# First row chunks of x as 64-row halves over two DMA queues, turned by half transposes, in a SwiGLU feed-forward kernel

## Chip, cores and metric

The kernel runs on one core of one Trainium2 chip. The metric is the device time of one execution in microseconds (us). The profiler's "span" runs from the first to the last instruction of the program; the time is a little longer than the span. Engines are called as in the profile: PE is TensorE's matmuls, PEld its weight loads, DVE is VectorE, ACT is ScalarE, POOL is GpSimd, SP is SyncE. SPq and ACTq are the DMA queues that SP and ACT issue to.

## What is computed

```python
# x: (1, 2048, 640), w_gate, w_up: (640, 1536), w_down: (1536, 640), all bf16
g = silu(x @ w_gate)
u = x @ w_up
return (g * u) @ w_down
```

## The kernel before

Rows of x are taken in four blocks of 512 (`S_BLK`), the 640 columns of x in five slices of 128 (`KD`, index `kd`), the 1536 hidden columns in twelve slices of 128 (`KF`, index `fc` or `kf`). The gate and up products need x with its columns on the partitions, which is the tile `xT`. For block `sb` and slice `fc`, `proj` (L202) runs five matmuls into a gate tile `pg` and five into an up tile `pu`, each 512 rows wide; `gate` (L217) takes the silu on ACT and the product on DVE into `aT`. After the twelve slices the down product reads `aT` and `wd_sb` (L287 and L316) and the result is copied and stored. PE runs these in the order of the program text, since `keep_order` (L100) ties all its instructions together; ACT, POOL, DVE and SP are ordered likewise.

The part that the change touches is the start, `head` (L226), and the loads ahead of it.

**Loads.** Only the first 256 rows of x, two chunks of 128 rows (`PE_X = 2`), are loaded as they are and turned on PE; rows 256 to 511 and the other blocks come turned by the DMA itself (`turn_x`, L110). Chunk 0 goes over SPq and chunk 1 over ACTq (L114, L115), 160 KB each. Then come the gate weights of the first four `fc` slices (`N_FIRST = 4`), one transfer of 128 KB for each `kd` (L120 to L122): `kd` 1 and 3 over ACTq (`ACT_K`), 0, 2 and 4 over SPq. After them SPq takes the up weights of the same four slices, `kd` 0 to 2 in one transfer of 384 KB and `kd` 3 and 4 in one of 256 KB (L123, L124), the two turning transfers for rows 256 to 511 (L125, L126), and the weights of the other slices (L128 to L131).

**PE in `head`.** First `warm` (L180) issues 20 matmuls of 128x128 on a tile of ones (`N_WARM`); their result is not used. Then `transpose_chunk` (L190) turns chunk 0 and chunk 1: five 128x128 transposes each (L195), the x tile as the weights and the identity as what streams. The transposes of `kd` 0 and 1 fill one PSUM tile, which ACT copies into `xT`; those of `kd` 2 to 4 fill another, which DVE copies (L200). Then come the gate pieces (L246 to L256). A piece is one `kd` and a range of rows, and each piece is four matmuls, one for each `fc`: `kd` 0 on chunk 0 (128 rows), `kd` 0 on chunk 1 (128 rows), then `kd` 1, 2, 3 and 4 on both chunks at once (256 rows). That makes 8 matmuls of 128 rows and 16 of 256. The up matmuls on the same 256 rows follow, 20 of them, in order of `kd` (L257 to L259); then gate and up on rows 256 to 511, which need the turning transfers (L260 to L265).

The up weights are called by their first transfer below: the 384 KB of `kd` 0 to 2 are what the first up matmul waits for.

Of the kernel before, what the change touches and what calls it, by code (L numbers as in the profile page):

```python
# [10 lines left out]
def _body(  # L11
# [8 lines left out]
    nc = tc.nc  # L20
    P = nc.NUM_PARTITIONS
    f32 = mybir.dt.float32
    bf16 = mybir.dt.bfloat16
# [9 lines left out]
    KD = D // P  # L33
# [3 lines left out]
    SUB = S_BLK // P  # L37
    DA = 512
    Q = 32
    N_WARM = 20  # L40
    T = 4
    WT_STEP = 4
    PE_X = 2
    ACT_K = (1, 3)
    X_CUT = 3
    N_FIRST = 4
    ROW_J = 0
# [6 lines left out]
    psum = ctx.enter_context(  # L54
        tc.tile_pool(name="psum", bufs=2, space=bass.MemoryType.PSUM)
    )

    ident = consts.tile([P, P], bf16)
    x_sb = consts.tile([P, PE_X, D], bf16)
    xT = consts.tile([P, KD, S], bf16)  # L60
# [14 lines left out]
    x_v = x2.rearrange("(c p) d -> p c d", p=P)  # L75
# [5 lines left out]
    def wslice(a, b):  # L81
        return slice(a * P, b * P)
# [4 lines left out]
    def load_x(eng, c0, c1):  # L87
        eng.dma_start(out=x_sb[:, c0:c1, :], in_=x_v[:, c0:c1, :])
# [11 lines left out]
    def keep_order(engine):  # L100

        traced = [i for i in nc.cur_bb.bb.instructions if i.engine == engine]
        for a, b in zip(traced, traced[1:]):
            issue_order(a, b)
# [6 lines left out]
        s_sl = slice(c0 * P, c1 * P)  # L111
        nc.sync.dma_start_transpose(out=xT[:, k0:k1, s_sl], in_=xt_v[s_sl, k0:k1])

    load_x(nc.sync, 0, 1)  # L114
    load_x(nc.scalar, 1, 2)  # L115
    def load_k(eng, dst, src, a, b, k0, k1):
        f_sl = wslice(a, b)
        eng.dma_start(out=dst[:, k0:k1, f_sl], in_=src[:, k0:k1, f_sl])

    for kd in range(KD):  # L120
        eng = nc.scalar if kd in ACT_K else nc.sync
        load_k(eng, wg_sb, wg_v, 0, N_FIRST, kd, kd + 1)  # L122
# [12 lines left out]
    def turn_w(dst, src):  # L135
# [7 lines left out]
        out=x_row[:],  # L143
        in_=x2[S - T : S, :].rearrange("t d -> (t d)").partition_broadcast(P),
# [35 lines left out]
    def warm(n):  # L180
        for _ in range(n):
            nc.tensor.matmul(  # L182
                pw[:, 0:P],
                lhsT=ones[:].broadcast_to([P, P]),
                rhs=ones[:].broadcast_to([P, P]),
                start=True,
                stop=True,
            )

    def transpose_chunk(c, parts):  # L190
        c_sl = slice(c * P, (c + 1) * P)
        for copy, tag, k0, k1 in parts:
            pt = psum.tile([P, k1 - k0, P], bf16, tag=tag, name="pt")
            for kd in range(k0, k1):
                nc.tensor.transpose(  # L195
                    out=pt[:, kd - k0, :],
                    in_=x_sb[:, c, kd * P : (kd + 1) * P],
                    identity=ident[:],
                )
            copy(out=xT[:, k0:k1, c_sl], in_=pt[:])  # L200

    def proj(ps, w_sb, fc, sb, c0, c1, k0=0, k1=KD):  # L202
        for kd in range(k0, k1):
            nc.tensor.matmul(  # L204
                ps[:, c0:c1],
                lhsT=w_sb[:, kd, fc * P : (fc + 1) * P],
                rhs=xT[:, kd, sb * S_BLK + c0 : sb * S_BLK + c1],
                start=(kd == 0),
                stop=(kd == KD - 1),
            )  # L210
# [6 lines left out]
    def gate(pg, pu, sb, fc, n_s):  # L217

        s0 = sb * S_BLK
        sg = work.tile([P, S_BLK], f32, name="sg")  # L220
        nc.scalar.activation(sg[:, 0:n_s], pg[:, 0:n_s], ACT.Silu)  # L221
        nc.vector.tensor_tensor(  # L222
            out=aT[:, fc, s0 : s0 + n_s], in0=sg[:, 0:n_s], in1=pu[:, 0:n_s], op=ALU.mult
        )

    def head():  # L226

        dve, act = nc.vector.tensor_copy, nc.scalar.copy
        split = [(act, "po_a", 0, 2), (dve, "po_b", 2, KD)]
        late = PE_X * P
        pgs = [
            psum.tile([P, S_BLK], f32, tag="gu", name="pg", bufs=4)
            for _ in range(N_FIRST)
        ]
        warm(N_WARM)
        transpose_chunk(0, split)  # L240
        transpose_chunk(1, split)
        pus = [
            psum.tile([P, S_BLK], f32, tag="po_a" if fc % 2 == 0 else "po_b", name="pu")
            for fc in range(N_FIRST)
        ]
        pieces = [(0, c * P, (c + 1) * P) for c in range(PE_X)]  # L246
        pieces += [(kd, 0, late) for kd in range(1, KD)]
        for kd, c0, c1 in pieces:
            for fc, pg in enumerate(pgs):
                nc.tensor.matmul(  # L250
                    pg[:, c0:c1],
                    lhsT=wg_sb[:, kd, wslice(fc, fc + 1)],
                    rhs=xT[:, kd, c0:c1],
                    start=(kd == 0 and c0 == 0),
                    stop=(kd == KD - 1),
                )  # L256
        for kd in range(KD):  # L257
            for fc, pu in enumerate(pus):
                proj(pu, wu_sb, fc, 0, 0, late, kd, kd + 1)  # L259
        for k0, k1 in ((0, X_CUT), (X_CUT, KD)):  # L260
            for fc, pg in enumerate(pgs):
                proj(pg, wg_sb, fc, 0, late, S_BLK, k0, k1)
        for fc, (pg, pu) in enumerate(zip(pgs, pus)):
            proj(pu, wu_sb, fc, 0, late, S_BLK)
            gate(pg, pu, 0, fc, S_BLK)  # L265
        keep_order(mybir.EngineType.PE)
        keep_order(mybir.EngineType.Activation)
        keep_order(mybir.EngineType.Pool)

    head()  # L270
    for sb in range(NSB):
        n_s = S_BLK if sb < NSB - 1 else S_BLK - T
# [26 lines left out]
        for q in range(P // Q):  # L299
            nc.scalar.dma_start(  # L300
                out=out2[
                    sb * S_BLK : sb * S_BLK + n_t, DA + q * Q : DA + (q + 1) * Q
                ].rearrange("(i r) c -> r i c", r=Q),
                in_=ot_q[q * Q : (q + 1) * Q, :].rearrange("r (i c) -> r i c", c=Q),
            )

        for j in range(SUB):
            s0 = sb * S_BLK + j * P
# [4 lines left out]
            for c0, c1, tag in cols:  # L313
# [10 lines left out]
                if c1 < D:  # L324
                    nc.scalar.copy(ot[:], po[:])  # L325
                    eng = nc.sync
                else:
                    nc.vector.tensor_copy(out=ot[:], in_=po[:])  # L328
                    eng = nc.sync
# [81 lines left out]
def kernel(tc, *args):  # L411
    _body(tc, *args)
    tc.close()
    tc.compile()
    _trim(tc.nc)
# [30 lines left out]
```

## Time and profile before

| what | value |
|---|---|
| time, median of 3 runs (lowest to highest) | 163.4 us (163.05 to 163.59) |
| time of the profiled execution | 163.25 us |
| span of the profiled execution | 161.9 us |
| PE busy | 159.6 us, 818 matmuls |
| DVE busy | 110.5 us |
| ACT busy | 42.6 us |
| DMA | 15.86 MB, of it 6.25 MB in the first 20 us |

The 1.35 us between span and time lie ahead of the first and behind the last instruction of the program. In a line of the chain or of the timeline the first number is the start in us from the beginning of the span and the second the length in us; "x4" is the number of instructions merged in the line. In a line of groups the figures behind the bar are the busy time in us, the mean duration of one instruction in ns, and the idle time of the engine ahead of them. A line of DMA issues ends with the time from issue to landing in us. A matmul's duration contains its way through the array, so that the matmuls of a stream overlap in the records: what one of them costs is the distance from start to start. A window of the timeline shows whatever runs in it, with the start of the first.

### The profile page before, as it was taken

The page shows a single profiled execution, that of the slowest core. Times are in us where ns is not written, and L with a number is a line of the kernel's source. Part 1 is how long each engine was busy: PE and PEld are TensorE (multiplying, and loading weights), DVE is VectorE, ACT ScalarE, POOL GpSimd, SP SyncE. Part 2 cuts the span into 40 slices and gives each one's busy share as a digit, 9 for nine tenths or more (in the row PEclk, how much of TensorE's full clock was granted, in tenths as well). Part 3 has the DMA queues.
Part 4 walks back from the last instruction along what each step waited for, and adds up shares of the span by engine and source line. Part 5 has one row for each costly group of instructions (what it writes and reads, how often), then busy time and mean ns, then how long its engine had stood idle before and what let it go on. Part 6 is the DMA issues. An engine that isn't in the chain of part 4 may idle for free.

```text
span 161.9 us, 2159 instructions
## 1 busy us (share of the span) xinstructions
PE 159.6 (99%) x818; PEld 79.9 (49%) x818; DVE 110.5 (68%) x249; ACT 42.6 (26%) x74; POOL 0.6 (0%) x6
## 2 busy tenths in 40 slices
PE   9999999999999999999999999999999999999995
PEld 9885444444444444444444444444444444445454
DVE  1006223599469999989919999979964999993000
ACT  5032222112222222211222322221214222222121
POOL 1000000000000000000000000000000000000000
PEclk9999999999999999999999999999999999999999
DMA  7999999995089992003110000000310000000212
GB/s 228 280 345 348 363 209 241 230 190 100 32 186 139 241 225 58 0 0 34 65 65 4 0 0 2 0 0 4 64 66 32 0 0 0 0 4 0 52 37 73
DMA packets 41209, 15.86 MB, mean 98 GB/s; under 512 B 33264, under 2 KB 41072, under 8 KB 41200
## 3 DMA queue, kind: packets, MB, share of 16 engines
q1 hardware_dynamic: 32832, 14.81, 38.0%
q10 hardware_dynamic: 8368, 0.92, 3.7%
q8 instruction: 6, 0.10, 0.3%
q14 instruction: 3, 0.02, 0.1%
HBM read 6.88 MB, written 2.62 MB: 59 GB/s over the span
## 4 chain that ended last, share of the span: by engine, by line
PE 99%; DVE 0%; issue 0%
PE pu L204 32%; PE pg L204 31%; PE po_a L316 26%; PE po_t L287 6%; PE pg L250 2%; PE pw L182 1%; PE pt L195 1%; DVE ot_b L328 0%; DVE ones L108 0%
## 5 line engine op out<-in xcount | busy, mean ns | idle before, releaser
L204 PE MATMUL pu<-xT,wu_sb 128*128 128x512 bf16 (+2 forms) x260 | 59.3, 362 | 0.0
L204 PE MATMUL pg<-xT,wg_sb 128*128 128x512 bf16 (+2 forms) x240 | 56.9, 370 | 0.0
L222 DVE TENSOR_TENSOR aT<-sg,pu 128x512 bf16<-128x512 f32 (+1 forms) x48 | 32.5, 682 | 32.8 <-PE pu L204 32.8
L221 ACT ACTIVATE sg<-pg 128x512 f32<-128x512 f32 (+1 forms) x48 | 28.4, 597 | 71.1 <-PE pg L204 67.5
L316 PE MATMUL po_a<-wd_sb,aT 128*128 128x512 bf16 (+2 forms) x216 | 42.8, 358 | 0.0
L153 DVE SCALAR_TENSOR_TENSOR prod<-wgT,x_row 128x640 f32<-128x640 bf16 x48 | 39.4, 821 | 1.1
L153 DVE SCALAR_TENSOR_TENSOR prod<-wuT,x_row 128x640 f32<-128x640 bf16 x48 | 39.4, 822 | 1.0
L204 PEld LDWEIGHTS <-wu_sb 128*128 128x128 bf16 x260 | 25.4, 98 | 26.5 <-DMA wu_sb<-in_w_up_dram 0.2
L204 PEld LDWEIGHTS <-wg_sb 128*128 128x128 bf16 x240 | 23.5, 98 | 25.9
L316 PEld LDWEIGHTS <-aT 128*128 128x128 bf16 x216 | 20.7, 98 | 21.6
L325 ACT CAST ot<-po_a 128x512 bf16<-128x512 f32 (+1 forms) x17 | 9.5, 561 | 32.0 <-PE po_a L316 20.9
L287 PE MATMUL po_t<-aT,wd_sb 128*128 128x512 bf16 (+1 forms) x48 | 10.4, 366 | 0.0
L287 PEld LDWEIGHTS <-wd_sb 128*128 128x128 bf16 x48 | 4.7, 98 | 5.1
L328 DVE CAST ot_b<-po_a 128x128 bf16<-128x128 f32 x1 | 0.3, 292 | 9.9 <-PE po_a L316 9.9
L296 ACT CAST ot_t<-po_t 128x512 bf16<-128x512 f32 (+1 forms) x4 | 2.2, 559 | 11.6 <-PE po_t L287 11.6
L153 DVE DVE_READ_ACCUMULATOR prod<-wuT,x_row 128x1 f32 x48 | 4.0, 82 | 0.0
L153 DVE DVE_READ_ACCUMULATOR prod<-wgT,x_row 128x1 f32 x48 | 3.9, 82 | 0.0
L298 DVE STREAM_TRANSPOSE ot_q<-ot_t 128x512 bf16<-128x512 bf16 (+1 forms) x4 | 2.7, 678 | 1.7 <-ACT ot_t L296 1.7
L250 PE MATMUL pg<-xT,wg_sb 128*128 128x256 bf16 (+1 forms) x24 | 3.1, 307 | 0.0
L200 DVE COPY xT<-pt 128x384 bf16<-128x384 bf16 x2 | 0.7, 358 | 3.2 <-PE pt L195 3.2
L250 PEld LDWEIGHTS <-wg_sb 128*128 128x128 bf16 x24 | 2.6, 127 | 0.3
L182 PE MATMUL pw<-ones 128*128 128x128 bf16 x20 | 2.3, 313 | 0.3 <-DVE ones L108 0.3
(15 smaller groups left out, 8.0 us busy)
## 6 DMA issues: line engine op xcount, KB each, us to landing
wd_sb<-in_w_down_dram SPq DMA_DIRECT2D x1, 1920.0 KB, 14.6
out_dram<-ot SPq DMA_DIRECT2D x15, 128.0 KB, 1.7
wg_sb<-in_w_gate_dram SPq DMA_DIRECT2D x2, 640.0 KB, 6.7
wu_sb<-in_w_up_dram SPq DMA_DIRECT2D x2, 640.0 KB, 8.0
x_row<-in_x_dram SPq DMA_DIRECT2D x1, 640.0 KB, 4.9
wg_sb<-in_w_gate_dram SPq DMA_DIRECT2D x3, 128.0 KB, 3.5
wu_sb<-in_w_up_dram SPq DMA_DIRECT2D x1, 384.0 KB, 4.7
out_dram<-ot_q ACTq DMA_DIRECT2D x12, 32.0 KB, 2.1
```

Of the source, the lines that this page charges most:

```text
L153: nc.vector.scalar_tensor_tensor(out=prod[:], in0=wT[:, fc, :], scalar=1.0, in1=x_row[:, t, :], op0=ALU.mult, op1=ALU.mult, accum_out=acc[ ...
L182: nc.tensor.matmul(pw[:, 0:P], lhsT=ones[:].broadcast_to([P, P]), rhs=ones[:].broadcast_to([P, P]), start=True, stop=True,)
L195: nc.tensor.transpose(out=pt[:, kd - k0, :], in_=x_sb[:, c, kd * P : (kd + 1) * P], identity=ident[:],)
L204: nc.tensor.matmul(ps[:, c0:c1], lhsT=w_sb[:, kd, fc * P : (fc + 1) * P], rhs=xT[:, kd, sb * S_BLK + c0 : sb * S_BLK + c1], start=(kd == 0 ...
L221: nc.scalar.activation(sg[:, 0:n_s], pg[:, 0:n_s], ACT.Silu)
L222: nc.vector.tensor_tensor(out=aT[:, fc, s0 : s0 + n_s], in0=sg[:, 0:n_s], in1=pu[:, 0:n_s], op=ALU.mult)
L250: nc.tensor.matmul(pg[:, c0:c1], lhsT=wg_sb[:, kd, wslice(fc, fc + 1)], rhs=xT[:, kd, c0:c1], start=(kd == 0 and c0 == 0), stop=(kd == KD ...
L287: nc.tensor.matmul(po_t[:], lhsT=wd_sb[:, kf, DA:D], rhs=aT[:, kf, sb * S_BLK : sb * S_BLK + n_t], start=(kf == 0), stop=(kf == KF - 1),)
L296: nc.scalar.copy(ot_t[:], po_t[:])
L298: nc.vector.transpose(out=ot_q[:], in_=ot_t[:])
L316: nc.tensor.matmul(po[:], lhsT=aT[:, kf, s0 : s0 + P], rhs=wd_sb[:, kf, c0:c1], start=(kf == 0), stop=(kf == KF - 1),)
L325: nc.scalar.copy(ot[:], po[:])
```

## The change

The two chunks are loaded as four transfers of 80 KB: of each chunk, rows 0 to 63 over SPq and rows 64 to 127 over ACTq. Gate weight `kd` 3 moves from ACTq to SPq. `transpose_chunk` now issues, for each `kd`, two transposes, one for each half of 64 rows; the halves stand in different row halves of the array (`tile_position` 0 and 64) and fill one PSUM tile each, of 5 x 64 columns. ACT copies the first half's tile into `xT`, DVE the second's, each after all five `kd`. The gate pieces are now `kd` 0 and `kd` 1 on chunk 0, `kd` 0 and `kd` 1 on chunk 1 (16 matmuls of 128 rows), then `kd` 2 to 4 on both (12 of 256 rows). 17 warm matmuls are issued in place of 20.

```diff
-    N_WARM = 20
+    N_WARM = 17
...
-    ACT_K = (1, 3)
+    ACT_K = (1,)
...
-    load_x(nc.sync, 0, 1)
-    load_x(nc.scalar, 1, 2)
+    for c in range(PE_X):
+        for eng, r0 in ((nc.sync, 0), (nc.scalar, P // 2)):
+            r_sl = slice(r0, r0 + P // 2)
+            eng.dma_start(out=x_sb[r_sl, c, :], in_=x_v[r_sl, c, :])
...
-    def transpose_chunk(c, parts):
-        c_sl = slice(c * P, (c + 1) * P)
-        for copy, tag, k0, k1 in parts:
-            pt = psum.tile([P, k1 - k0, P], bf16, tag=tag, name="pt")
-            for kd in range(k0, k1):
+    def transpose_chunk(c, copies):
+        h_rows = P // len(copies)
+        pts = [
+            psum.tile([P, KD, h_rows], bf16, tag=tag, name="pt") for _, tag in copies
+        ]
+        for kd in range(KD):
+            for h, pt in enumerate(pts):
+                h_sl = slice(h * h_rows, (h + 1) * h_rows)
                 nc.tensor.transpose(
-                    out=pt[:, kd - k0, :],
-                    in_=x_sb[:, c, kd * P : (kd + 1) * P],
-                    identity=ident[:],
+                    out=pt[:, kd, :],
+                    in_=x_sb[h_sl, c, kd * P : (kd + 1) * P],
+                    identity=ident[h_sl, h_sl],
+                    tile_position=(h * h_rows, 0),
                 )
-            copy(out=xT[:, k0:k1, c_sl], in_=pt[:])
+        for h, (copy, _) in enumerate(copies):
+            s0 = c * P + h * h_rows
+            copy(out=xT[:, :, s0 : s0 + h_rows], in_=pts[h][:])
...
-        split = [(act, "po_a", 0, 2), (dve, "po_b", 2, KD)]
+        split = [(act, "po_a"), (dve, "po_b")]
...
-        pieces = [(0, c * P, (c + 1) * P) for c in range(PE_X)]
-        pieces += [(kd, 0, late) for kd in range(1, KD)]
+        pieces = [(kd, c * P, (c + 1) * P) for c in range(PE_X) for kd in range(2)]
+        pieces += [(kd, 0, late) for kd in range(2, KD)]
```

## The prediction

> **What bounds the kernel now.** I read the chain of waits first. Its summary of the whole span by engine:
>
> ```profile
> PE 99%; DVE 0%; issue 0%
> ```
>
> PE is never short of work for long, so whatever the start gains or loses comes out at the end one for one, and nothing behind the start has slack to absorb it. So I read PE's timeline over the first 10 us:
>
> ```profile
> 0.30 2.31 PE L182 MATMUL pw<-ones 128*128 128x128 bf16 x20 [0.30 <-DVE ones L108]
> 2.41 1.27 PE L195 MATMUL pt<-ident,x_sb 128*128 128x128 bf16 x10
> 3.48 3.13 PE L250 MATMUL pg<-xT,wg_sb 128*128 128x128 bf16 x24
> 6.57 2.36 PE L204 MATMUL pu<-xT,wu_sb 128*128 128x256 bf16 x20
> 8.76 1.47 PE L204 MATMUL pg<-xT,wg_sb 128*128 128x256 bf16 x12
> ```
>
> Ten transposes take 3.48 - 2.41 = 1.07 us, 0.107 each. The change must be judged at one place: the first up matmul at 6.57. Behind it PE runs without a break; ahead of it stands the only wait of the stage, in the timeline of the weight loads:
>
> ```profile
> 6.56 2.08 PEld L204 LDWEIGHTS <-wu_sb 128*128 128x128 bf16 x20 [0.23 <-DMA wu_sb<-in_w_up_dram]
> ```
>
> PE stood for 0.23 us until the first up weights landed. The stage is thus held by the DMA, by a little, and PE work saved ahead of 6.57 is lost in that wait. When the data lands follows from when it is issued, in the timeline of SP and of ACT,
>
> ```profile
> 0.00 0.40 SPq L88 DMA_DIRECT2D x_sb<-in_x_dram  x1
> 0.45 1.36 SPq L118 DMA_DIRECT2D wg_sb<-in_w_gate_dram  x3
> 1.86 1.22 SPq L118 DMA_DIRECT2D wu_sb<-in_w_up_dram  x2
> 3.12 2.59 SPq L112 DMA_TRANSPOSE xT<-in_x_dram  x2
> ```
>
> ```profile
> 0.12 0.39 ACTq L88 DMA_DIRECT2D x_sb<-in_x_dram  x1
> 0.55 0.93 ACTq L118 DMA_DIRECT2D wg_sb<-in_w_gate_dram  x2
> ```
>
> and the time from issue to landing, in the DMA issues of the first 20 us and, for the first gate transfer of each queue and the first turning transfer, in narrow windows of the same view:
>
> ```profile
> wu_sb<-in_w_up_dram SPq DMA_DIRECT2D x1, 384.0 KB, 4.7
> ...
> x_sb<-in_x_dram SPq DMA_DIRECT2D x1, 160.0 KB, 2.1
> x_sb<-in_x_dram ACTq DMA_DIRECT2D x1, 160.0 KB, 2.6
> ```
>
> ```profile
> wg_sb<-in_w_gate_dram SPq DMA_DIRECT2D x1, 128.0 KB, 2.8
> ```
>
> ```profile
> wg_sb<-in_w_gate_dram ACTq DMA_DIRECT2D x1, 128.0 KB, 3.5
> ```
>
> ```profile
> xT<-in_x_dram SPq DMA_TRANSPOSE x1, 4.9
> ```
>
> Chunk 0 lands at 2.1, chunk 1 at 0.12 + 2.6 = 2.7, gate kd 0 at 0.45 + 2.8 = 3.25, gate kd 1 at 0.55 + 3.5 = 4.05, the first up weights at 1.86 + 4.7 = 6.56, the first turned rows at 3.12 + 4.9 = 8.0.
>
> **The price of a matmul in this stage.** The profile's clock column shows 1.00 here, but the spacing does not. Narrow windows of PE's timeline give the starts of 256-row gate matmuls, and the groups of 159 to 159.9 us give the 128-row matmuls at the end of the kernel:
>
> ```profile
> 4.54 0.64 PE L250 MATMUL pg<-xT,wg_sb 128*128 128x256 bf16 x2
> 4.76 0.54 PE L250 MATMUL pg<-xT,wg_sb 128*128 128x256 bf16 x2
> ...
> 5.25 0.60 PE L250 MATMUL pg<-xT,wg_sb 128*128 128x256 bf16 x4
> 5.36 0.60 PE L250 MATMUL pg<-xT,wg_sb 128*128 128x256 bf16 x4
> ```
>
> ```profile
> L316 PE MATMUL po_a<-wd_sb,aT 128*128 128x128 bf16 x12 | 0.8, 219 | 0.0
> ```
>
> Until about 5.1 us PE runs at half rate: 256 rows cost 0.213 (by the rows 0.22), 128 rows 0.107. After it 256 rows cost 0.109 and 128 rows some 0.056 (0.8 less one duration of 0.22, over 11 steps).
>
> **Part by part.**
>
> Three warm matmuls less: 3 x 0.107 = 0.32 us earlier at PE, so the first transpose could start at 2.09 in place of 2.41. That is only worth something if x is there. The first half's 80 KB over SPq lands by 2.1 at the latest, where 160 KB does now. The second half goes over ACTq, issued at 0.12. Its bounds are 1.9 (SP's 2.1, less 0.3 for 80 KB fewer at the stage's rate, below, plus 0.12) and 2.7 (where ACT's 160 KB land now). I take 2.2, between them and nearer to SP's row, since half the bytes are asked for: the transposes start at 2.2.
>
> The half transposes: 20 in place of 10, each with a weight load of 128 columns from 64 rows and a stream of 64 columns. No such form is in this trace. The nearest rows, from the groups by form of the first 16 us, with the copies:
>
> ```profile
> L204 PEld LDWEIGHTS <-wg_sb 128*128 128x128 bf16 x30 | 2.9, 98 | 1.2
> ...
> L195 PEld LDWEIGHTS <-x_sb 128*128 128x128 bf16 x10 | 1.1, 151 | 0.0
> ...
> L200 ACT COPY xT<-pt 128x256 bf16<-128x256 bf16 x2 | 0.7, 364 | 0.1
> L200 DVE COPY xT<-pt 128x384 bf16<-128x384 bf16 x2 | 0.7, 358 | 3.2 <-PE pt L195 3.2
> ```
>
> A load's duration falls from 151 to 98 ns where the rate doubles: 53 ns, as much as 128 columns save in a matmul (0.107 to 0.056). So a load seems to take 0.107 at half rate by itself. Lower bound for a pair of halves: 0.053, both streams side by side and the loads hidden, 0.53 us for all. Upper: loads one after the other, 20 x 0.107 = 2.14 us, and a pipeline emptied at each end of the stage, 2 x 0.2 (ten transposes take 1.27 us to the last one's end, 0.31 beyond nine steps of 0.107; less one step). I take 0.107 a pair, 1.07 us in all as now: the halves use different rows of the array, and the load of one pair is as long as a full load is today. The Trainium skill, TensorEngine Tiling (Array Packing), section Tiling Modes, speaks for the middle and for a surcharge: tiles in different rows can load and multiply in parallel, but changing the tiling mode drains TensorE; by that the sum would be 1.07 plus up to 0.4. The trace of before has no change of mode that could show it.
>
> The copies: 5 x 64 = 320 columns each, between the 256 of ACT's row and the 384 of DVE's, so about 0.4 and 0.35 us. They now wait for all of a chunk's transposes. Chunk 0 is turned at 2.2 + 0.53 + some 0.3 until its result stands = 3.05, copied at 3.45. Chunk 1's transposes cover this; without that cover it would cost 0.4.
>
> So the first gate matmul starts at about 3.5, as now (3.48): what three warm matmuls give back goes into the wait for x and for the copies. Gate kd 0 lands no later: 160 KB of x stand ahead of it on SPq, in one transfer or two. It is issued some 0.45 later, at 0.9, but even at x's 2.1 us it would be there by 3.0, ahead of the 3.25 that its bytes allow.
>
> The gate pieces: kd 1 moves from the ninth matmul to the fifth. Four at 0.107 from 3.5 end at 3.93. Gate kd 1 has the same 160 KB ahead of it on ACTq as now, so it lands at 4.05 again, and with its load PE starts it at about 4.17: a new wait of 0.24 us. Everything in PE's order is queued behind it. Its bounds are none (gate kd 1 at 3.8, half-way to kd 0's 3.25, since its bytes are then done sooner) and 0.6 (4.5, one ACT issue of 0.45 later). Then 12 matmuls of 128 rows: 8.7 of them until 5.1, the other 3.3 at 0.056 until 5.28; 12 of 256 rows at 0.109 until 6.59. Splitting kd 1 costs nothing: two 128-row matmuls at 0.107 are one of 256 at 0.213, and at the full rate 2 x 0.056 against 0.109. PE is ready for the up weights at 6.59 in place of about 6.45 (6.57 less most of its wait); the wait for them covers the difference.
>
> The queues: two more transfers, and SP issues two more ahead of the up weights (an x half and gate kd 3), 2 x 0.46. They are issued at 2.8 in place of 1.86. The bytes ahead of them are the same. From an empty queue 384 KB would need 2.1 plus 224 KB at the rate below, 0.6, and land at 5.5; so the late issue is hidden by the queue, and costs at most 0.9 if the queue ran empty. The DMA rate in the stretches from 1 to 6 us (last column GB/s, first and last of the four slow ones, and the fast one):
>
> ```profile
> 1.00:2.00 1.00, 1.00 (x13) 1.00 (x11) 0.00 (x0) 0.49 (x1) 0.00 (x0) 1.00 0.96 297
> ...
> 4.00:5.00 1.00, 1.00 (x10) 0.81 (x8) 0.08 (x1) 0.00 (x0) 0.00 (x0) 1.00 1.02 286
> 5.00:6.00 1.00, 1.00 (x10) 0.91 (x9) 0.00 (x0) 0.00 (x0) 0.00 (x0) 1.00 1.09 375
> ```
>
> Seven transfers of 128 to 160 KB run at some 290 GB/s, the 384 KB at 375. If each small transfer costs a pause, that is 4 us x (1 - 290/375) / 7 = 0.13 each, and two more cost 0.26. If it is the mixing of two queues that costs, ACTq is done with 288 KB in place of 416 and the up weights come earlier by up to 0.2 (one slow stretch of 286 at 375 is 0.24 shorter). I take +0.1: landing at 6.66.
>
> The turning transfers are issued 0.9 later, at 4.0. By their bytes they land at 8.0, by their issue at 8.9; PE needs them at 8.76 + 0.1. That hides all but 0.05.
>
> Sum: the first up matmul at 6.67 in place of 6.57, **+0.1 us**. The profiled execution took 163.25 (span 161.9 and 1.35 around it), so 163.35; the median of the runs shown is 0.15 higher, 163.4, which makes **163.5 us**. About 0.3%, 0.5 us, is what a measurement of this kernel can tell from no change.
>
> **Rivals.**
>
> The loads run in series (slower). Twenty loads at 0.107 from 2.2 end at 4.34. By 5.1, 7 of the 16 small gate matmuls are done; 9 x 0.056 and 12 x 0.109 end at 6.91: +0.34, and with a drained pipeline at each end (0.4 at half rate, worth 0.2 at the full one, and more if the first 64-row load waits on ACTq till 2.7) up to +0.75. Median 163.75 to 164.15. It decides as soon as a pair costs more than about 0.13, since PE has only 0.1 us to give. For it: the load row of 151 ns; against it: disjoint rows. The Trainium skill, TensorE: Matmul & The Clock Gate, section LDWEIGHTS, says that a load's time goes by columns and not by rows, so halving the rows would double the load work; the 53 ns above agrees with the columns, and the rows of the array are not tried here.
>
> The half rate lasts longer (slower). PE doubled at 5.1, after 4.8 us of unbroken full-size matmuls. If idle time at 2.1, 3.4 and 3.95 and half-filled transposes make that count begin again at 3.5, the doubling comes at 8.3, and 3.2 us at half rate cost 1.6: about 165.0. Against it: the pauses are 0.1 to 0.25 us. The same skill page, Part 1, has a free-running window of about 3.4 us that must be busy; a missed window would then cost some 1.7.
>
> Gate kd 1 lands at 4.5 (slower, small): 5.5 matmuls until 5.1, 6.5 x 0.056 and 1.31 end at 6.77: +0.2, 163.6; it decides from 4.1 on.
>
> The up weights land 0.2 earlier (faster), halves side by side at 0.53: PE is ready at about 6.4, -0.15, 163.2. More would need both PE and DMA half a microsecond earlier.
>
> The halves of x land no earlier than now: PE waits until 2.4 in place of warming, and the copies, gate kd 1 and the up weights still come last: 163.5 to 163.6, within the forecast.
>
> **How the numbers follow.** Forecast with the unmoved x halves 0.47 (163.3 to 163.7), loads in series 0.25, gate kd 1 late 0.10, longer half rate 0.08, faster 0.10. Slower by over 0.3% (above 163.9): 0.15 of the serial loads, 0.08 of the half rate, 0.04 of the late gate weights, 0.05 of the forecast by its upper bounds: 0.32. Faster (below 162.9): 0.05 of the faster rival and 0.02 of the forecast, 0.07. Within: 0.61. The range, 163.0 to 164.2, takes in the forecast, the serial loads with drains and half of the faster rival, and leaves out the long half rate.
>
> **What would show it.** The first up matmul at 6.5 to 6.8 with its weights as the last to land; twenty half transposes over about 1.1 us; the first gate matmul near 3.5 and a gap ahead of the fifth; the spacing of 256 rows at 0.109 from about 5.1 on. Transposes over 2 us, or 0.213 spacing beyond 5.5, speak for the slower rivals. I am wrong if the up weights land before 6.3 or after 7.0.

## The result and the profile after

The changed kernel takes 165.52 us (median of 6 runs, 165.27 to 166.13) against 163.5 for the kernel before (163.05 to 163.94): a ratio of 1.0131, 95% interval [1.0115, 1.0148]. It is slower by 2.0 us; 163.5 was forecast, with a range up to 164.2. The profiled execution took 165.27 us with a span of 163.9, so the whole difference lies inside the span (161.9 before).

PE's timeline over the first 12 us of the changed kernel, to be laid beside the five lines that the prediction shows of before (L200 are now the transposes, L258 the gate pieces, L212 the later gate and up matmuls):

```profile
0.31 1.99 PE L184 MATMUL pw<-ones 128*128 128x128 bf16 x17 [0.31 <-DVE ones L108]
2.26 0.94 PE L200 MATMUL pt<-ident,x_sb 64*128 64x64 bf16 x11
3.57 0.45 PE L200 MATMUL pt<-ident,x_sb 64*128 64x64 bf16 x9 [0.38 <-DMA x_sb<-in_x_dram]
4.16 4.47 PE L258 MATMUL pg<-xT,wg_sb 128*128 128x128 bf16 x28
8.50 2.44 PE L212 MATMUL pu<-xT,wu_sb 128*128 128x256 bf16 x20
10.78 1.47 PE L212 MATMUL pg<-xT,wg_sb 128*128 128x256 bf16 x12
```

The first up matmul starts at 8.50 in place of 6.57, 1.93 us later, and the rest of the kernel is moved by that much. Two things are late ahead of it: the first gate matmul (4.16 in place of 3.48), and the gate pieces themselves, which now last to the up matmuls at 8.50. The waits of the weight loads, in the same stretch:

```profile
2.25 0.10 PEld L200 LDWEIGHTS <-x_sb 64*128 64x128 bf16 x1 [0.22 <-DMA x_sb<-in_x_dram]
2.60 0.47 PEld L200 LDWEIGHTS <-x_sb 64*128 64x128 bf16 x10 [0.24 <-DMA x_sb<-in_x_dram]
3.57 0.29 PEld L200 LDWEIGHTS <-x_sb 64*128 64x128 bf16 x9 [0.50 <-DMA x_sb<-in_x_dram]
4.15 3.99 PEld L258 LDWEIGHTS <-wg_sb 128*128 128x128 bf16 x28 [0.29 <-DMA wg_sb<-in_w_gate_dram]
8.50 2.17 PEld L212 LDWEIGHTS <-wu_sb 128*128 128x128 bf16 x20 [0.35 <-DMA wu_sb<-in_w_up_dram]
```

Every load that PE needs is now waited for: both halves of chunk 0, chunk 1, the first gate weights, the up weights. The timelines of SP and of ACT say where that begins:

```profile
0.00 1.20 SPq L117 DMA_DIRECT2D x_sb<-in_x_dram  x2
1.24 2.01 SPq L120 DMA_DIRECT2D wg_sb<-in_w_gate_dram  x4
3.29 0.96 SPq L120 DMA_DIRECT2D wu_sb<-in_w_up_dram  x2
```

```profile
0.14 1.35 ACTq L117 DMA_DIRECT2D x_sb<-in_x_dram  x2
1.53 0.60 ACTq L120 DMA_DIRECT2D wg_sb<-in_w_gate_dram  x1
2.16 1.28 ACT L129 ACT_TABLE_LOAD   x1 [2.16 <-issue]
```

Issuing a half of 80 KB takes 0.60 us (1.20 for two), longer than the 0.40 of a whole chunk, and the first gate transfer behind the halves takes 0.59 where it took 0.41 before. SP comes to its first gate transfer at 1.24 in place of 0.45, and to the up weights at 3.29 in place of 1.86. From there the DMA issues of the first 20 us show

```profile
wu_sb<-in_w_up_dram SPq DMA_DIRECT2D x1, 384.0 KB, 5.2
```

so the up weights land at 3.29 + 5.2 = 8.5. Their 1.93 us of delay are 0.79 from the two x issues, 0.64 from the gate issues (four in 2.05 us in place of three in 1.41) and 0.5 from a longer way to landing (4.7 before). The DMA rates of four stretches, to be read against the 297 and 375 GB/s of before in 1 to 2 and 5 to 6 us:

```profile
1.00:2.00 1.00, 1.00 (x13) 1.00 (x10) 0.00 (x0) 0.00 (x0) 0.00 (x0) 1.00 0.53 155
2.00:3.00 1.00, 0.89 (x14) 0.46 (x12) 0.00 (x0) 0.84 (x1) 0.00 (x0) 1.00 0.87 251
...
5.00:6.00 1.00, 1.00 (x11) 1.00 (x10) 0.00 (x0) 0.00 (x0) 0.00 (x0) 1.00 0.69 181
6.00:7.00 1.00, 1.00 (x7) 0.69 (x6) 0.00 (x0) 0.00 (x0) 0.00 (x0) 1.00 0.98 318
```

The last column but one is the DMA engines' busy share. At 0.53 and 0.69 they stood idle for a good part of the time, twice; the second time the up weights had been issued since 3.29. Before, the share was 0.95 or more in each of these stretches up to 6 us.

PE has a trouble of its own. Narrow windows of its timeline around 8 us give the starts of the 256-row matmuls, gate pieces first and up matmuls behind them:

```profile
7.78 0.63 PE L258 MATMUL pg<-xT,wg_sb 128*128 128x256 bf16 x2
7.99 0.63 PE L258 MATMUL pg<-xT,wg_sb 128*128 128x256 bf16 x2
...
8.69 0.51 PE L212 MATMUL pu<-xT,wu_sb 128*128 128x256 bf16 x3
8.82 0.49 PE L212 MATMUL pu<-xT,wu_sb 128*128 128x256 bf16 x3
```

The spacing is still 0.21 at 8 us and falls only at about 8.7. Before, it fell at 5.1. Between 2.1 and 4.16 PE had only the twenty half transposes to do, some 0.5 us by the distance from start to start (priced below), and so idled for over a microsecond. So there are two explanations of the same 1.9 us, and this one trace can't tell them apart, because PE was through its gate pieces at half rate (8.2 + 0.21) just as the up weights landed.

### The profile page after: what moved, and what is told of

Same layout as the page of the kernel before. It is cut to its first block, busy times and chain, and to the rows that moved or that the text cites. A ratio compares the mean times of both kernels' runs of the same rounds, so it can differ in the third digit from the quotient of the medians.

```text
span 163.9 us, 2184 instructions
## 1 busy us (share of the span) xinstructions
PE 161.0 (98%) x829; PEld 80.1 (49%) x829; DVE 110.5 (67%) x249; ACT 42.7 (26%) x74; POOL 0.6 (0%) x6
## 4 chain that ended last, share of the span: by engine, by line
PE 96%; DMA 2%; SPq 1%; DVE 0%; issue 0%
PE pu L212 32%; PE pg L212 30%; PE po_a L324 26%; PE po_t L295 6%; PE pg L258 3%; DMA wg_sb<-in_w_gate_dram 2%; SPq L117 1%; DVE ot_b L336 0%
## 5 line engine op out<-in xcount | busy, mean ns | idle before, releaser
L212 PE MATMUL pu<-xT,wu_sb 128*128 128x512 bf16 (+2 forms) x260 | 59.4, 363 | 0.0
L212 PE MATMUL pg<-xT,wg_sb 128*128 128x512 bf16 (+2 forms) x240 | 56.9, 370 | 0.0
L212 PEld LDWEIGHTS <-wu_sb 128*128 128x128 bf16 x260 | 25.4, 98 | 26.7 <-DMA wu_sb<-in_w_up_dram 0.4
L212 PEld LDWEIGHTS <-wg_sb 128*128 128x128 bf16 x240 | 23.5, 98 | 25.9
L258 PE MATMUL pg<-xT,wg_sb 128*128 128x128 bf16 (+1 forms) x28 | 4.5, 358 | 0.1
L258 PEld LDWEIGHTS <-wg_sb 128*128 128x128 bf16 x28 | 3.3, 145 | 1.0 <-DMA wg_sb<-in_w_gate_dram 0.3
L208 DVE COPY xT<-pt 128x320 bf16<-128x320 bf16 x2 | 0.7, 325 | 3.5 <-PE pt L200 3.5
```

The lines of the kernel that those rows point to most:

```text
L212: nc.tensor.matmul(ps[:, c0:c1], lhsT=w_sb[:, kd, fc * P : (fc + 1) * P], rhs=xT[:, kd, sb * S_BLK + c0 : sb * S_BLK + c1], start=(kd == 0 ...
L258: nc.tensor.matmul(pg[:, c0:c1], lhsT=wg_sb[:, kd, wslice(fc, fc + 1)], rhs=xT[:, kd, c0:c1], start=(kd == 0 and c0 == 0), stop=(kd == KD ...
```

## The experiments

The **loads theory** says that the x halves and the longer SP queue make the up weights late, and that this alone sets the time. The **clock theory** says that PE's idle time keeps it at half rate, and that the time would be as long with the weights there. A third, the **turning theory**, blames the half transposes or the new order of the pieces. Ratios are to the kernel before, with 95% intervals.

**The new PE side on the old loads.**

```diff
# against the changed kernel
-    ACT_K = (1,)
+    ACT_K = (1, 3)
-    for c in range(PE_X): ...two halves of 64 rows, over SP and ACT
+    load_x(nc.sync, 0, 1)
+    load_x(nc.scalar, 1, 2)
```

> The changed kernel's PE side (half transposes, gate pieces in the new order, 17 warm matmuls) on the loads of before (whole chunks of x, gate kd 1 and 3 over ACTq). Loads theory: the 64-row transfers make every later transfer late, so here the first up weights land at 6.5 again and the time is 163.2 to 163.6. Clock theory: PE has no long idle time with these loads, so the rate doubles near 5.1 and the time is 163.2 to 163.6 too. Turning theory (the half transposes or the new order cost the two microseconds): 165 to 166.

Measured: 164.77 us, 1.0088 [1.0054, 1.0123], with a wide spread (163.59 to 165.23). None of the three bands holds the median. The profiled execution is the fastest of the four, 163.59; its PE timeline:

```profile
2.23 0.90 PE L198 MATMUL pt<-ident,x_sb 64*128 64x64 bf16 x20
3.37 2.80 PE L256 MATMUL pg<-xT,wg_sb 128*128 128x128 bf16 x28 [0.24 <-ACT xT L206]
6.91 2.36 PE L210 MATMUL pu<-xT,wu_sb 128*128 128x256 bf16 x20 [0.74 <-DMA wu_sb<-in_w_up_dram]
```

There the 28 gate matmuls took 2.80 us, so the rate had doubled early, and PE waited 0.74 for the up weights (at 6.9, issued at 1.86 as before). In the executions of 165, of which there is no trace, something else must have been late; the same kernel kept busy, further below, says what.

**The old PE side on the new loads.**

```diff
# against the kernel before
-    ACT_K = (1, 3)
+    ACT_K = (1,)
-    load_x(nc.sync, 0, 1)
-    load_x(nc.scalar, 1, 2)
+    for c in range(PE_X): ...the changed kernel's four half loads
```

> The PE side of before (20 warm matmuls, whole transposes, old order of the pieces) on the loads of the changed kernel. Loads theory: first up weights at 8.3 to 8.6, time 165.2 to 165.7. Clock theory: PE idles only some 0.8 us ahead of the first gate matmul, the time is 164.3 to 165.7, and the half rate lasts to the end of the gate pieces. Turning theory: 163.4 to 163.7.

Measured: 165.32 us, 1.0114 [1.0092, 1.0136]: the new loads alone give nearly all of the loss. PE's timeline:

```profile
4.13 3.07 PE L252 MATMUL pg<-xT,wg_sb 128*128 128x128 bf16 x24
8.57 2.36 PE L206 MATMUL pu<-xT,wu_sb 128*128 128x256 bf16 x20 [1.37 <-DMA wu_sb<-in_w_up_dram]
```

Here PE was through its gate pieces at 7.2 and then idled for 1.37 us. The gate pieces lasted about as long as before (3.07 us against 3.13), so the half rate had ended early here. The up weights come at 8.5 all the same, and SP's two half loads take 1.20 us to issue as in the changed kernel. The turning theory is out as the cause of the two microseconds, and so is the clock as their only cause.

**The changed kernel with PE kept busy.**

```diff
# against the changed kernel
-    N_WARM = 17
+    N_WARM = 22
...
         transpose_chunk(0, split)
+        warm(8)
         transpose_chunk(1, split)
+        warm(4)
```

> The changed kernel with its PE idle time filled: 22 warm matmuls ahead, 8 between the two chunks' transposes, 4 behind them; no load is touched. Loads theory: the rate doubles near 5 us, PE is through the gate pieces before 7.3, waits over a microsecond for the up weights at 8.4, and the time stays at 165.2 to 165.6. Clock theory: the up weights matter little, the time falls to 163.6 to 164.2.

Measured: 165.41 us, 1.0113 [1.0083, 1.0143]. PE's timeline, last gate pieces and first up matmul:

```profile
6.19 1.05 PE L260 MATMUL pg<-xT,wg_sb 128*128 128x256 bf16 x8 [0.18 <-DMA wg_sb<-in_w_gate_dram]
8.72 2.36 PE L212 MATMUL pu<-xT,wu_sb 128*128 128x256 bf16 x20 [1.48 <-DMA wu_sb<-in_w_up_dram]
```

Eight matmuls in 1.05 us: full rate, and PE done by 7.24. It gains nothing, since it now waits 1.48 us. In the changed kernel the half rate is hidden behind the late weights (8.50 there, 8.7 here).

**Idle time alone.**

```diff
# against the kernel before
-    N_WARM = 20
+    N_WARM = 2
```

> The kernel of before with 2 warm matmuls in place of 20, so PE idles from 0.6 to 2.3 us; no load is touched. Loads theory: the up weights land at 6.5 as before; if the rate doubles as before, 163.4 to 163.6. Clock theory: the doubling comes 1 to 3.4 us later and the time is 164.2 to 165.2.

Measured: 164.5 us over ten runs from 163.38 to 166.13, 1.0058 [1.0032, 1.0084]. PE's timeline of the profiled execution (164.12):

```profile
3.57 4.06 PE L250 MATMUL pg<-xT,wg_sb 128*128 128x128 bf16 x24 [0.16 <-ACT xT L200]
7.46 2.35 PE L204 MATMUL pu<-xT,wu_sb 128*128 128x256 bf16 x20
```

With the loads untouched (up weights at 1.85 + 4.6 = 6.45) the same 24 gate matmuls last 4 us in place of 3.13, and the up matmuls begin at 7.46 without a wait. The spacing of 256 rows stays at 0.21 until 6.8 here; some 0.3 us more went into a wait for gate weights at 4.69. So idle time ahead can cost PE its rate, and the times differ widely between executions. The clock theory is right as a mechanism; it is not what set the changed kernel's time. The Trainium skill, TensorE: Matmul & The Clock Gate, Part 1, has a free-running activity window, whose phase differs from run to run. The spread of 2.7 us over ten runs agrees in kind, though it is more than the 1.7 that the prediction works out for one missed window.

**The same four transfers by columns.**

```diff
# against the kernel before; ACT_K = (1,) as well
-    load_x(nc.sync, 0, 1)
-    load_x(nc.scalar, 1, 2)
+    for c in range(PE_X):
+        for eng, d0 in ((nc.sync, 0), (nc.scalar, D // 2)):
+            d_sl = slice(d0, d0 + D // 2)
+            eng.dma_start(out=x_sb[:, c, d_sl], in_=x_v[:, c, d_sl])
```

> The PE side of before; x again in four transfers of 80 KB, two on each queue, but each of 128 rows by 320 columns in place of 64 rows by 640; gate kd 3 over SPq as in the changed kernel. Shape theory (the 64 rows make the issue slow, 0.57 us in place of 0.40): an issue takes 0.40 to 0.45, the first up weights land at 7.0 to 7.5, time 163.8 to 164.4. Number theory (four transfers and the longer SP queue are the cost, whatever their shape): up weights at 8.3 to 8.6, time 165.1 to 165.6.

Measured: 165.79 us, 1.0142 [1.0123, 1.016]. SP's timeline:

```profile
0.00 0.87 SPq L117 DMA_DIRECT2D x_sb<-in_x_dram  x2
0.91 1.85 SPq L120 DMA_DIRECT2D wg_sb<-in_w_gate_dram  x4
2.81 0.96 SPq L120 DMA_DIRECT2D wu_sb<-in_w_up_dram  x2
```

Neither theory has all of it. With 128 rows an issue does take 0.44 in place of 0.60, so the slow issue belongs to the 64-row shape. But the time is no better: the up weights still land 5.3 us behind their issue, at 8.1, and the first gate matmul waited for its weights until 4.62, longer than in the changed kernel. PE's gate pieces then last at half rate to 8.86:

```profile
4.62 4.45 PE L252 MATMUL pg<-xT,wg_sb 128*128 128x128 bf16 x24 [0.87 <-DMA wg_sb<-in_w_gate_dram]
8.86 2.56 PE L206 MATMUL pu<-xT,wu_sb 128*128 128x256 bf16 x20
```

So the start is set by PE here: late gate weights, and the half rate behind them, with the up weights there 0.8 us before they are used. Column halves on the same queues are no way out; what they would cost with the rate doubled was not run.

**Gate kd 3 alone, both ways.** First the kernel before with `ACT_K = (1,)`, then the changed kernel with `ACT_K = (1, 3)`.

> The kernel of before with one edit: gate kd 3 goes over SPq in place of ACTq. It issues the up weights one SP issue later, at 2.3 in place of 1.86. If moving this transfer is a part of the loss: up weights at 6.9 to 7.5, time 163.8 to 164.4. If the loss comes from the x halves alone: 163.3 to 163.6.

> The changed kernel with gate kd 3 back on ACTq. The up weights are issued at 2.8 in place of 3.3. If the x halves alone make the loss: still 165.0 to 165.6. If gate kd 3 on SPq has a part in it: up weights at 7.5 to 8.0; the time is then set by PE's half rate and lies between 164.3 and 165.2.

Measured: 163.97 us, 1.0034 [1.0018, 1.005], for the first, with the up weights issued at 2.33 and landing at 6.9, 4.6 later; 165.4 us, 1.0122 [1.0102, 1.0142], for the second, with up weights at 2.94 + 5.1 = 8.0. So this small edit costs about 0.5 us by itself on the old loads. How much of that the later weights make isn't shown, since PE's timeline has no wait for them:

```profile
3.49 3.73 PE L250 MATMUL pg<-xT,wg_sb 128*128 128x128 bf16 x24
7.05 2.35 PE L204 MATMUL pu<-xT,wu_sb 128*128 128x256 bf16 x20
```

The gate pieces kept the spacing of 0.21 until about 6.3, in place of 5.1, and ended only as the weights landed. PE had no more idle time ahead than in the kernel before, so idle time is not all that moves the doubling. On the new loads, taking the edit back gains nothing: the weights come half a microsecond earlier, but ACT issues one transfer more, its first copy into `xT` begins at 4.05 in place of 3.56 and the first gate matmul at 4.51; the half rate then lasts until the first up matmul at 8.63.

**The new PE side on the old loads, kept busy.**

```diff
# against the first experiment
-    N_WARM = 17
+    N_WARM = 18
...
         transpose_chunk(0, split)
+        warm(2)
         transpose_chunk(1, split)
+        warm(4)
```

> The first experiment (the changed PE side on the loads of before) with its idle time filled: 18 warm matmuls ahead, 2 between the chunks, 4 ahead of the gate pieces. Clock theory (the half transposes leave PE idle, and the doubling comes later in many executions): 163.1 to 163.7 and all executions close together. Turning theory (the half transposes or the new order cost by themselves): 164.3 to 165, as without the filling.

Measured: 163.85 us, twelve runs within 163.32 to 164.16, 1.002 [1.0006, 1.0034]. Seven more matmuls made it 0.9 us faster than the first experiment and took the spread away: what was late there was, in all likelihood, the doubling of PE's rate. A median 0.15 above the expected band is left; in the profiled execution the up weights, issued at 1.86 as before, landed at 6.96, some 0.4 later than before. PE's timeline prices the half transposes:

```profile
2.44 0.45 PE L198 MATMUL pt<-ident,x_sb 64*128 64x64 bf16 x10
2.83 0.40 PE L182 MATMUL pw<-ones 128*128 128x128 bf16 x2
```

Ten halves from first start to last end in 0.45 us: less the 0.24 that one lasts (236 ns in the changed kernel's groups), 0.21 over nine steps, 0.05 a pair. The next full-size matmul starts 0.18 behind the last half.

**Issues without bytes.**

```diff
# against the kernel before, ahead of the first up weights
+    for n in range(2):
+        scr = consts.tile([P, Q], bf16, name=f"scr{n}")
+        nc.sync.dma_start(out=scr[:], in_=x_v[:, 8 + n, 0:Q])
```

> The kernel of before with two transfers of 8 KB that nobody reads issued on SPq just ahead of the first up weights: two issues more, hardly a byte more. Issue theory (the up weights land a fixed time behind their issue): issued at 2.7, they land at 7.3 to 7.8, time 164.0 to 164.8. Byte theory (they land when the bytes ahead of them are through, as the prediction had it): 6.5 to 6.8, time 163.4 to 163.7.

Measured: 164.87 us, 1.0081 [1.0059, 1.0102]. SP's timeline, PE's line of the first up matmul, and the DMA rate ahead of it:

```profile
1.86 1.35 SPq L125 DMA_DIRECT2D scr<-in_x_dram  x2
3.25 0.96 SPq L118 DMA_DIRECT2D wu_sb<-in_w_up_dram  x2
```

```profile
8.01 2.36 PE L207 MATMUL pu<-xT,wu_sb 128*128 128x256 bf16 x20 [1.29 <-DMA wu_sb<-in_w_up_dram]
```

```profile
4.25:5.25 1.00, 1.00 (x9) 0.76 (x7) 0.00 (x0) 0.00 (x0) 0.00 (x0) 1.00 0.66 83
5.25:6.25 1.00, 1.00 (x12) 0.90 (x10) 0.00 (x0) 0.00 (x0) 0.00 (x0) 1.00 0.89 274
```

Sixteen KB more, and the up weights land at 3.25 + 4.7 = 7.95, 1.4 us later, by just the delay of their issue. The rate falls to 83 GB/s from 4.25 on, with the engines busy for 0.66 of the time: little is left of what was issued earlier, and the transfer that was issued at 3.25 brings bytes in number only two microseconds later. This decides between issue and bytes for a later issue: the landing moves with it, though hardly a byte was added.

The issue was expected at 2.7 and came at 3.25, since SP's own waits show this:

```profile
SPq L125 <- DMA x_sb<-in_x_dram: 0.6, 1, 0.6
```

SP stood 0.6 us ahead of the second small transfer until a chunk of x had landed; in the kernel before it stood 0.4 so ahead of the second up transfer, with no wait of PE behind it. Why an issue waits for x is not shown, and the changed kernel has no such wait. So of the 1.4 us some 0.6 is this wait and the rest the two issues.

**Issuing the up weights earlier.** The kernel before with gate kd 4 on ACTq too (`ACT_K = (1, 3, 4)`, with DVE and ACT changing places in the copies), and with one transfer fewer:

```diff
# the second of the two, against the kernel before
-    for kd in range(KD): ...one transfer for each kd, over SP or ACT
+    for eng, k0, k1 in ((nc.sync, 0, 1), (nc.scalar, 1, 2), (nc.scalar, 2, 3), (nc.sync, 3, KD)):
+        load_k(eng, wg_sb, wg_v, 0, N_FIRST, k0, k1)
```

> The kernel of before with gate kd 4 moved to ACTq as well (kd 1, 3 and 4 there), so SP issues the up weights one issue earlier, at 1.4; DVE copies the transposes of kd 0 and 1 and ACT the others, since ACT is busy with the issue 0.45 us longer. Issue theory: up weights land at 6.0 to 6.3, PE is ready for them at 6.4 or later, time 162.9 to 163.4. Byte theory: 6.5 to 6.9, time 163.4 to 163.9.

> The kernel of before with one transfer fewer: gate kd 3 and 4 in one of 256 KB over SPq, kd 2 over ACTq behind kd 1. SP issues the up weights at 1.4. Issue theory: up weights at 6.0 to 6.3, time 162.9 to 163.4. Byte theory: 6.5 to 6.8, no change, 163.3 to 163.7.

Measured: 163.86 us, 1.0014 [1.0001, 1.0027], and 164.17 us, 1.0041 [1.0027, 1.0055]. The issue theory misses here. Issued at 1.4, the up weights land at 7.5 and 6.9, no earlier than before, and PE now waits about a microsecond for gate weights that come later:

```profile
5.86 1.21 PEld L249 LDWEIGHTS <-wg_sb 128*128 128x128 bf16 x12 [1.28 <-DMA wg_sb<-in_w_gate_dram]
```

(the weight loads of the second). So there is a floor under the issue theory: an earlier issue than 1.86 does not bring an earlier landing. The bytes ahead are the likeliest floor, and by that both limits lie close together in the kernel before; this is argued, not shown, since around 4 to 4.5 us the engines were not fully busy in these runs either (shares of 0.73 and 0.78).

**A cut that moves bytes behind the wait.**

```diff
# against the kernel before
-    load_k(nc.sync, wu_sb, wu_v, 0, N_FIRST, 0, X_CUT)
-    load_k(nc.sync, wu_sb, wu_v, 0, N_FIRST, X_CUT, KD)
+    load_k(nc.sync, wu_sb, wu_v, 0, N_FIRST, 0, 2)
+    load_k(nc.sync, wu_sb, wu_v, 0, N_FIRST, 2, KD)
```

> The kernel of before with the up weights cut after kd 1 in place of kd 2: the first transfer is 256 KB, the second 384 KB; number and time of the issues stay. If the 128 KB less are what the wait ahead of the first up matmul hangs on: the first transfer lands near 6.1, PE does not wait, the second (needed 0.9 us behind the first up matmul) is just in time, time 163.2 to 163.5 against 163.5 of before. If the landing hangs on the issue alone: 6.5 again and no change, 163.4 to 163.7.

Measured: 163.48 us against 163.69 for the kernel before in the same runs, 0.998 [0.9965, 0.9995]: a gain of 0.2%, with an interval that barely leaves out no change. The mechanism isn't shown: the profiled execution, at 163.82, was the slowest of the twelve, held up by the first gate weights.

## Why the prediction was wrong, step by step

**What bounds the kernel** was read rightly: the first up matmul is the place, and its weights are the last to land, before and after. The delay there, 1.93 us, came out at the end almost one for one (2.0).

**The queues** are the step that failed. It said that "the late issue is hidden by the queue, and costs at most 0.9 if the queue ran empty". It priced the two issues at 0.46 each and took a landing at 6.66. Measured: 8.5. The size of the issues was off: an x half takes 0.60, not 0.40 to 0.46, and holds up what follows, so the up weights were issued at 3.29, not 2.8. And the cover was not there: 16 KB in two transfers, with no other edit, put the issue off by 1.4 us and the landing by as much. The fault in the argument was to read most of a transfer's 4.7 us from issue to landing as waiting behind other bytes, and to allow it 2.7 (2.1 and 0.6) from an empty queue; with the engines partly idle ahead of it, it took 4.7 as well. The time stayed at 4.6 to 5.1 on whole chunks wherever the issue stood between 1.85 and 3.25 (the kernel before and five experiments), and at 5.1 to 5.4 on the split ones. The bound that was named, +0.9 if the queue ran empty, got no rival and no chance of its own, and lies outside the stated range (163.4 and 0.9 are 164.3). Even it was too low, by 0.5 of slower issues and 0.5 of a longer landing. The +0.1 that was taken in its place came from a pause for each small transfer, a term that no run shows by itself.

**Gate kd 0**, said to land "no later" at 3.25, landed at 1.24 + 2.87 = 4.11 by the chain of waits: the same mistake, earlier in the queue.

```profile
1.24 2.87 DMA wg_sb<-in_w_gate_dram
4.11 0.05 issue
4.16 4.47 PE pg L258 x28
```

**The x halves**: first transposes at 2.26 against 2.2 forecast, but the second half came at 2.60 and chunk 1 at 3.57, 0.9 later than the 2.7 of before; the forecast had only the first chunk in doubt.

**The half transposes** were over-priced: 0.107 a pair was taken, 0.05 was measured, the lower bound. The rival of loads in series is refuted by the same figure: two loads of 128 columns in 0.05 us do not stand one behind the other. The rule of the Trainium skill that tiles in different rows can load and multiply in parallel (TensorEngine Tiling (Array Packing), Tiling Modes) agrees; of the drain at a change of mode there is at most the 0.18 above.

**The copies** were right in length (0.42 and 0.33 by the mean of L208). Their start was not: ACT began the first at 3.56 in place of 3.05, because its issues moved its table load of 1.28 us from 1.51 to 2.16. It ended just ahead of gate kd 0, so that the gate pieces could not have begun before about 4.0 even with their weights there. Splitting kd 1 cost nothing at half rate, as said: from 4.16, sixteen matmuls at 0.107 and twelve at 0.213 end at 8.43, which is where PE stood (8.2 + 0.21).

**The half rate** was a rival at 0.08 with the doubling at 8.3 and 165.0 us. The doubling did come at 8.7. It happened, and it hurts by itself (the first and fourth experiments), but in the changed kernel it is hidden: without it, 165.41. Its time of 165.0 is near the measured one by luck. What sets the doubling is not settled: in the profiled executions it had come by 3.8 with the new loads and the old PE side, for all the idle time there, and at 6.3 with gate kd 3 alone moved and no idle time.

Left open: why 64 rows, and the transfer behind them, take longer to issue, why the up weights land some 0.5 us later behind their issue with split loads than with whole ones (means of 5.2 and 4.8), and whether the queue or the engines hold a transfer back for two microseconds. No run here tells these apart.

## What to carry to other kernels

Count DMA issues on each queue ahead of the transfer that the first dense stage waits for, and price them as time, not only as bytes: here no backlog hid them. A transfer's time from issue to landing is not proof of a queue ahead of it. Nor is a high DMA busy share: the kernel before showed 0.95 or more in each stretch up to 6 us, and a later issue still moved the landing in full. Adding transfers with hardly a byte told it. And idle time on PE in the first microseconds can cost twice, once as idle time and once more as a longer stretch at half rate, as with 2 warm matmuls here.

## What the runs showed of the hardware beyond this

Two half transposes in different row halves cost 0.05 us a pair at PE's half rate, against 0.107 for one whole transpose: half the time for the same data. A DMA issue of 64 rows by 1280 bytes took 0.60 us on SP, one of 128 rows by 640 bytes 0.44, the same 80 KB. Two microseconds of warm-up matmuls ahead were worth 0.6% of the time, and much of the evenness between executions: beside the first four experiments twelve of 13 runs with 20 such matmuls lay within 163.11 to 163.91 (one at 165.74), the ten runs with 2 of them within 163.38 to 166.13.
